# A delta-rule attention kernel: the inner outputs of six chunks by pairs of batches, their masks on GpSimd

## The chip, the cores and the metric

The kernel runs on one core of a Trainium2 chip. The metric is the device time of one execution in microseconds (us); the time given for a kernel is the median of several executions. A profile is one further execution, recorded by the hardware.

## The reference

Two stages. The first is a delta-rule attention over 4 batches, 8 heads, 768 steps and a head of 48:

```python
for t in range(S):
    kt, vt, bt = (k_n[:, :, t], v[:, :, t], beta[:, :, t, None])
    y[:, :, t] = np.einsum('bhd,bhde->bhe', q[:, :, t], state)
    v_old = np.einsum('bhde,bhd->bhe', state, kt)
    state = state + bt[:, :, :, None] * np.einsum('bhd,bhe->bhde', kt, vt - v_old)
```

(`k_n` are the keys divided by their norms.) The second stage takes the 3072 rows of 384 that come out, routes each to one of 16 experts (a group of 4 by argmax, then one of its 4), and computes `combined * (relu(x @ w1) @ w2)` with that expert's weights. Everything is float32.

## The kernel before

The attention is done in 24 chunks of 32 steps. All four batches are worked on at once: partition `b * 32 + t` holds step t of batch b. Within a chunk the recurrence is solved by the inverse of a triangular 32x32 matrix; such inverses are made on VectorE for a group of four chunks at a time (`inverse(g)`, lines 392 and 398 being its products and additions), transposed (L428), and spread into a factor `mtb` that is zero between the two batches of a pair (L437 on VectorE, L439 on ScalarE). Group g serves chunks 4g to 4g + 3; the last, group 5, is spread by VectorE alone.

Chunk u is `advance(u)`. On TensorE it multiplies the state with the keys (`a_ps`, L495) and with the queries (`o_ps`, L504), the factor with that (`w_ps`, L512), then updates the state (`s_ps`, L523), which ScalarE copies back in two pieces into `s_bd` (L529); the next chunk's `a_ps` waits for them. Last comes the inner output: the masked products of the chunk's queries and keys (`gq`) times `w`, added to `o_ps`; ScalarE copies the sum to `x` (L546). `logits(u - 1)` (L564, L465) turns the previous chunk's `x` and multiplies it with the router's weights, and `route` works on the logits of a group of chunks: on GpSimd `acc` (L613), the steps from `rk` to `cw` (L655 to L663), `what` (L701), `mine` (L706) and four `at` (L647), which TensorE uses one per chunk in the sorting matmul (L729).

The products of queries and keys are made by `gram` ten chunks ahead (`LEAD` = 10), so those of chunk 23 are made during chunk 13, and from chunk 14 (`LATE`) on TensorE has none left to make. `mask(u)` sets to zero what lies on or after the diagonal. For most chunks it writes 64 columns for each head, the chunk's own 32 and 32 zeros for the other batch of its pair, so that one matmul of 64x64 serves two batches (16 matmuls a chunk, L537). For chunks 14 to 19 (`halved`) it writes only the 32 (128x256 instead of 128x512, L294 instead of L298), and 32 matmuls of 32x32 are made (L542). All masks are VectorE's.

The transposed keys and queries of chunk u lie in `kqt_[u % 12]`, keys in half 0, queries in half 1; `load_kq(u + 12)` fills the buffer again at the end of period u, for the last time for chunk 23 in period 11.

The order of the instructions on every engine is that in which the program issues them: the main loop over `u` issues a period, and between its steps `work(n)` and `allow(...)` issue pieces of the inverses and of the routing. Nothing is reordered afterwards; an engine runs its own list in order and waits where an instruction needs another engine's result. A mask is issued at the start of the period before its chunk (`mask(u + 1)`).

The expert stage follows: TensorE takes the 16 experts one after another while their weights are loaded and rows are gathered and scattered by GpSimd's DMAs.

Of the kernel before, what the change touches and what calls it, by code (L numbers as in the profile page):

```python
# [9 lines left out]
F32 = mybir.dt.float32  # L10
I32 = mybir.dt.int32
AX = mybir.AxisListType
ALU = mybir.AluOpType
# [3 lines left out]
C = 32  # L17
RG = 4
# [48 lines left out]
def deltanet_then_moe(  # L67
# [13 lines left out]
    nc = tc.nc  # L81
    B, H, S, D = shape
    NP = H // 2
    NCH = S // C
# [15 lines left out]
    quads = [slice(b * C, (b + 1) * C) for b in range(B)]  # L100
    pairs = [slice(0, 64), slice(64, 128)]
# [9 lines left out]
    cut = {name: con[:, a:b] for name, (a, b) in const_at.items()}  # L111
# [65 lines left out]
    with ExitStack() as first:  # L177
        ap_ = first.enter_context(tc.tile_pool(name="attn", bufs=1))
        wk = first.enter_context(tc.tile_pool(name="wk", bufs=2))
# [10 lines left out]
        NB, NV = LEAD + 2, 3  # L190
        LATE, SMALL, KR = NCH - LEAD, NGR - 1, 64 + D
        ENDING = NCH - 2
        halved = range(LATE, SMALL * RG)
        kqt_ = [ap_.tile([128, 2, NP, 128], F32, name=f"kqt{i}") for i in range(NB)]
        kv_ = [ap_.tile([128, NP * KR + H * D], F32, name=f"kv{i}") for i in range(NV)]

        def load_kq(u, a=None):
            half = slice(0, 2) if a is None else slice(a, a + 1)
            nc.sync.dma_start(out=kqt_[u % NB][0:KR, half],
                              in_=kq_d[u].rearrange("p (a j t) -> p a j t", a=2, j=NP)[:, half])  # L200
# [36 lines left out]
        gts, raws, gqs, mts, norm, vhs, xs, turned_over = {}, {}, {}, {}, {}, {}, {}, set()  # L237
# [49 lines left out]
        def mask(u):  # L287

            like = [128, H, 2, C]
            gqm = wk.tile(like, F32, tag="gqm", name=f"gqm{u}", bufs=3)  # L290
            if u in halved:
                gqs[u] = gqm.rearrange("p h a t -> p (h a t)")[:, 0:H * C].rearrange(
                    "p (h t) -> p h t", t=C)
                nc.vector.tensor_tensor(gqs[u], raws.pop(u), cut["causal"][:, None, :].to_broadcast(  # L294
                    [128, H, C]), op=ALU.mult)
                return
            gqs[u] = gqm
            nc.vector.tensor_tensor(  # L298
                gqs[u], raws.pop(u)[:, :, None, :].to_broadcast(like),
                cut["upper"].rearrange("p (a t) -> p a t", a=2)[:, None].to_broadcast(like),  # L300
                op=ALU.mult)
# [182 lines left out]
        def advance(u):  # L484

            g, uu = divmod(u, RG)
            kqt = kqt_[u % NB]
            k = kv_[u % NV][:, 0:NP * KR].rearrange("p (j d) -> p j d", j=NP)
            if u == 0:
                f = vhs.pop(u)  # L490
            else:
                a_ps = begun_with.pop(u)
                for j in range(NP):
                    for b in range(B):
                        nc.tensor.matmul(a_ps[quads[b], 2 * j:2 * j + 2, :],  # L495
                                         lhsT=kqt[0:KR, 0, j, quads[b]], rhs=s_bd[0:KR, b, j],
                                         start=False, stop=True, skip_group_check=True)
                f = wk.tile([128, H, D], F32, tag="f", name=f"f{u}")
                nc.scalar.activation(f, a_ps, ACT.Copy)
            o_ps = ps.tile([128, H, D], F32, tag="o", name=f"o_ps{u}")  # L500
            if u > 0:
                for j in range(NP):
                    for b in range(B):
                        nc.tensor.matmul(o_ps[quads[b], 2 * j:2 * j + 2, :],  # L504
                                         lhsT=kqt[0:KR, 1, j, quads[b]], rhs=s_bd[0:KR, b, j],
                                         start=(j == 0), stop=False, skip_group_check=True)
            yield
            mt = mts[g]
            w_ps = ps.tile([128, H, D], F32, tag="s", name=f"w_ps{u}")
            for h in range(H):  # L510
                for b in pairs:
                    nc.tensor.matmul(w_ps[b, h], lhsT=mt[b, uu * H + (h % 2) * NP + h // 2],  # L512
                                     rhs=f[b, h], start=(h == 0), stop=True,
                                     skip_group_check=True)
            w = wk.tile([128, H, D], F32, tag="w", name=f"w{u}")
            nc.scalar.activation(w, w_ps, ACT.Copy)
            yield


            if u < NCH - 1:  # L520
                for j in range(NP):
                    for b in range(B):
                        nc.tensor.matmul(s_at[0:KR, b, j], lhsT=k[quads[b], j, 0:KR],  # L523
                                         rhs=w[quads[b], 2 * j:2 * j + 2],
                                         start=(u == 0 and j == 0), stop=True,
                                         skip_group_check=True)
                for hh in range(2):
                    rows = slice(hh * 64, hh * 64 + D)
                    nc.scalar.activation(s_bd[rows, :, :, hh, :],  # L529
                                         s_at[rows, :, :, hh * D:(hh + 1) * D], ACT.Copy)  # L530
            yield
            gq = gqs.pop(u)
            for h in range(H):
                hq = (h % 2) * NP + h // 2
                if u not in halved:
                    for b in pairs:
                        nc.tensor.matmul(o_ps[b, h], lhsT=gq[b, hq].rearrange("p a t -> p (a t)"),  # L537
                                         rhs=w[b, h], start=(u == 0 and h == 0), stop=True,
                                         skip_group_check=True)
                else:  # L540
                    for b in range(B):
                        nc.tensor.matmul(o_ps[quads[b], h], lhsT=gq[quads[b], hq],  # L542
                                         rhs=w[quads[b], h], start=False, stop=True,
                                         skip_group_check=True)
            x = wk.tile([128, DM], F32, tag="x", name=f"x{u}", bufs=4)
            nc.scalar.activation(x, o_ps.rearrange("p h d -> p (h d)"), ACT.Copy)  # L546
            xs[u] = x
            yield
# [251 lines left out]
        with tc.manual_schedule(engines={mybir.EngineType.PE, mybir.EngineType.DVE,  # L800
# [34 lines left out]
            for n in (H * D, H * D):  # L835
                nc.tensor.matmul(s_ps[:, 0, 0:n], lhsT=ident, rhs=con[:, cols[1]:cols[1] + n],
                                 start=True, stop=True, skip_group_check=True)
            second = inverse(1)
            start(second, 0.95)
            while 0 not in mts:  # L840
                work(4)
                allow(ACT_STEP)
            mask(0)
            scale(1)
            allow(ROOTS)
# [50 lines left out]
            for u in range(NCH + 1):  # L896
                step = advance(u) if u < NCH else iter([None] * 4)
                turned = logits(u - 1) if u else iter([None] * 2)
                if 0 < u < NCH - 1:
                    mask(u + 1)  # L900
                if u == 2:
                    scale(RG)
# [80 lines left out]
                work(12)  # L983
                if u == 0:
                    mask(1)
                if 0 < u < NCH - NB:
                    load_kq(u + NB)
                if u < NCH - NV:
# [265 lines left out]
    with tc.For_i(0, n_over):  # L1254
# [23 lines left out]
                                op=ALU.mult)  # L1278
# [71 lines left out]
```

## Time and profile before

| | us |
|---|---|
| median of 3 executions | 498.28 (496.32 to 499.61) |
| profiled execution | 490.29 |
| its span (first to last instruction) | 488.5 |
| busy: TensorE | 446.1 (91%) |
| busy: VectorE | 241.9 (50%) |
| busy: ScalarE | 189.5 (39%) |
| busy: GpSimd | 187.1 (38%) |

In the profile PE is TensorE's matmuls, PEld its loading of weights, DVE VectorE, ACT ScalarE, POOL GpSimd; "issue" is time in which an engine waited for nothing that the profile shows. A float32 matmul of the program leaves two records on PE and two on PEld. The mean granted clock of TensorE was 0.994 of full speed. The chain of work that ended last passes through TensorE for 34% of the span, VectorE for 19%, DMA for 18%.

### The profile page before, as it was taken

What the parts mean: (1) busy time and instruction counts of PE and PEld (TensorE: products, weight loads), DVE (VectorE), ACT (ScalarE), POOL (GpSimd) and SP (SyncE); (2) the same over time, 40 slices, a digit from 0 to 9 for tenths busy, and PEclk for the clock granted to TensorE, in tenths of its full rate; (3) what the DMA queues carried; (4) which work ended last, traced back from release to release, by engine and by line L of the source; (5) the groups of instructions that cost most, each with busy time, mean ns of one, the idle gap of its engine ahead of it and who ended that gap; (6) DMA issues with size and microseconds to landing.
All of it is one profiled execution on the core that took longest, in us unless ns stands there. A gap on an engine that the chain in (4) does not pass through costs nothing.

```text
span 488.5 us, 18022 instructions
## 1 busy us (share of the span) xinstructions
PE 446.1 (91%) x7674; PEld 421.8 (86%) x7674; DVE 241.9 (50%) x890; ACT 189.5 (39%) x407; POOL 187.1 (38%) x322
## 2 busy tenths in 40 slices
PE   3447999989999999999999999999999999999992
PEld 3335888878888889889999999999999999999992
DVE  4999999999999995474101210220122011201110
ACT  2327888777877776532112111111211111111110
POOL 0040310634517124103455445545735365256122
PEclk9999999999999999999999999999999999999997
DMA  5567455444355542207977877958987898778740
GB/s 164 150 185 237 135 149 179 143 127 146 102 160 173 174 126 98 63 19 197 372 230 238 285 228 215 312 160 282 326 268 232 264 326 302 230 220 305 262 133 30
DMA packets 56741, 97.06 MB, mean 199 GB/s; under 512 B 18958, under 2 KB 41417, under 8 KB 56659
## 3 DMA queue, kind: packets, MB, share of 16 engines
q1 hardware_dynamic: 50739, 85.89, 55.3%
q0 software_dynamic: 5920, 10.00, 6.7%
q8 instruction: 61, 1.00, 0.9%
q14 instruction: 21, 0.17, 0.1%
HBM read 81.75 MB, written 14.27 MB: 197 GB/s over the span
## 4 chain that ended last, share of the span: by engine, by line
PE 34%; DVE 19%; DMA 18%; issue 12%; POOL 8%; ACT 4%; SPq 3%; POOLq 0%; DVEq 0%
PE h_ps L1115 7%; PE y_ps L1134 7%; DMA out_dram<-yo,to_i 7%; DMA y_dram<-yq 6%; POOL xq L1087 6%; DVE m L398 5%; DVE below L392 4%; PE w_ps L512 4%; DMA yr<-y_dram 4%; SPq L1174 2%; PE a_ps L495 2%; PE o_ps L537 2%; PE s_ps L523 2%; PE o_ps L504 2%; POOL out_dram L1146 2%
## 5 line engine op out<-in xcount | busy, mean ns | idle before, releaser
L1134 PE MATMUL y_ps<-hid,w 128*128 128x224 f32 (+15 forms) x768 | 132.2, 331 | 0.0
L1134 PEld LDWEIGHTS y_ps<-hid,w 128*128 128x128 f32 x768 | 129.0, 190 | 0.3
L1115 PE MATMUL h_ps<-xt,w 128*128 128x232 f32 (+14 forms) x720 | 122.7, 330 | 0.0
L1115 PEld LDWEIGHTS h_ps<-xt,w 128*128 128x128 f32 x720 | 120.1, 190 | 0.3
L1087 POOL DMA_INDIRECT xq<-x_dram,from_q x92 | 87.9, 955 | 34.7 <-issue 24.8
L1137 DVE COPY yt<-y_ps 128x232 f32<-128x232 f32 (+13 forms) x14 | 5.1, 366 | 133.3 <-PE y_ps L1134 133.3
L1118 ACT ACTIVATE hid<-h_ps 128x448 f32<-128x448 f32 (+15 forms) x64 | 32.1, 502 | 100.2 <-PE h_ps L1115 100.2
L1146 POOL DMA_INDIRECT out_dram<-yo,to_i x32 | 34.3, 1073 | 92.8 <-DVE yo L1184 82.1
L1139 ACT ACTIVATE yt<-y_ps 128x224 f32<-128x224 f32 (+15 forms) x34 | 11.4, 337 | 116.6 <-PE y_ps L1134 116.6
L398 DVE TENSOR_TENSOR m<-m,below 128x16 f32<-128x16 f32 (+4 forms) x180 | 53.6, 298 | 0.4
L392 DVE TENSOR_TENSOR below<-m 128x16 f32<-128x16 f32 (+4 forms) x180 | 52.1, 292 | 0.1
L529 ACT ACTIVATE s_bd<-s_ps 48x768 f32<-48x768 f32 x46 | 37.0, 805 | 5.4 <-PE s_ps L523 4.8
L1184 DVE TENSOR_SCALAR yo<-yr,gate 128x384 f32<-128x384 f32 (+14 forms) x28 | 11.2, 415 | 53.0 <-DMA yr<-y_dram 44.0
L512 PEld LDWEIGHTS w_ps<-f,mtb 64*64 64x64 f32 x736 | 23.5, 134 | 5.6 <-issue 2.7
L512 PE MATMUL w_ps<-f,mtb 64*64 64x48 f32 x736 | 26.7, 220 | 1.4 <-issue 0.9
L439 ACT ACTIVATE mtb<-mt,con 128x256 f32<-128x256 f32 x35 | 25.5, 744 | 1.1 <-DVE mt L428 1.1
L274 PE MATMUL g_ps<-kqt 48*32 48x64 f32 (+1 forms) x1152 | 16.8, 236 | 9.3 <-DMA kqt<-in_kq_dram 7.7
L523 PE MATMUL s_ps<-w,kv 32*112 32x96 f32 x736 | 24.3, 267 | 0.9 <-issue 0.5
L613 POOL TENSOR_TENSOR acc<-acc,hots 128x16 f32<-128x16 f32 x16 | 4.2, 260 | 53.1 <-DVE hots L611 52.1
L537 PE MATMUL o_ps<-w,gqm 64*64 64x48 f32 x576 | 21.2, 220 | 3.2 <-issue 3.1
L523 PEld LDWEIGHTS s_ps<-w,kv 32*112 32x112 f32 x736 | 20.4, 172 | 3.2 <-issue 0.7
L274 PEld LDWEIGHTS g_ps<-kqt 48*32 48x32 f32 x1152 | 13.4, 114 | 11.0 <-issue 6.6
(186 smaller groups left out, 581.8 us busy)
## 6 DMA issues: line engine op xcount, KB each, us to landing
w<-in_w_dram SPq DMA_DIRECT2D x29, 1536.0 KB, 8.3
kv<-in_kv_dram SPq DMA_DIRECT2D x24, 416.0 KB, 3.8
kqt<-in_kq_dram SPq DMA_DIRECT2D x20, 448.0 KB, 4.4
x_dram<-x SPq DMA_DIRECT2D x24, 192.0 KB, 2.5
w<-in_w_dram SPq DMA_DIRECT2D x24, 128.0 KB, 3.1
y_dram<-yq SPq DMA_DIRECT2D x36, 84.0 KB, 9.7
yr<-y_dram SPq DMA_DIRECT2D x14, 192.0 KB, 2.4
kqt<-in_kq_dram SPq DMA_DIRECT2D x8, 224.0 KB, 3.3
```

The lines of the kernel that those rows point to most:

```text
L274: nc.tensor.matmul(g_out[quads[b], hh * NP + j, of], lhsT=kqt[rows, 0, j, quads[b]], rhs=kqt[rows, of, j, quads[b]], start=True, stop=True ...
L392: nc.vector.tensor_tensor(t, column.to_broadcast(like), row.to_broadcast(like), op=ALU.mult)
L398: nc.vector.tensor_tensor(to, to, t, op=ALU.add)
L512: nc.tensor.matmul(w_ps[b, h], lhsT=mt[b, uu * H + (h % 2) * NP + h // 2], rhs=f[b, h], start=(h == 0), stop=True, skip_group_check=True)
L523: nc.tensor.matmul(s_at[0:KR, b, j], lhsT=k[quads[b], j, 0:KR], rhs=w[quads[b], 2 * j:2 * j + 2], start=(u == 0 and j == 0), stop=True, sk ...
L529: nc.scalar.activation(s_bd[rows, :, :, hh, :], s_at[rows, :, :, hh * D:(hh + 1) * D], ACT.Copy)
L537: nc.tensor.matmul(o_ps[b, h], lhsT=gq[b, hq].rearrange("p a t -> p (a t)"), rhs=w[b, h], start=(u == 0 and h == 0), stop=True, skip_group ...
L1087: nc.gpsimd.indirect_dma_start(out=xq[:, g, :], out_offset=None, in_=x_dram[:, :].rearrange("n (q c) -> (n q) c", q=4), in_offset=bass.Ind ...
L1115: nc.tensor.matmul(h_ps[:, k], lhsT=w1[:, j, (f + k) * 128:(f + k + 1) * 128], rhs=xt[:, j, 0:R], start=(j == 0), stop=(j == DC - 1), skip ...
L1118: nc.scalar.activation(hid[:, f:f + 2], h_ps, ACT.Relu)
L1134: nc.tensor.matmul(y_ps, lhsT=w2[:, f, j * 128:(j + 1) * 128], rhs=hid[:, f], start=(f == 0), stop=(f == FC - 1))
L1146: put = nc.gpsimd.indirect_dma_start(out=out[:, :], out_offset=bass.IndirectOffsetOnAxis(ap=to[0:P, i:i + 1], axis=0), in_=yo[0:P, :], in_ ...
```

## The change

For chunks 14 to 19 the masks get the full width of 128x512, are made by GpSimd instead of VectorE, and are issued at the end of the period two before their chunk. They are written into the key half of `kqt_[(u - 2) % 12]`, the buffer of chunk u - 2, into which nothing is loaded any more. The inner outputs of these chunks are made like those of the others, by 16 matmuls of 64x64.

```diff
-        halved = range(LATE, SMALL * RG)
+        ahead_masks, SOONER = range(LATE, SMALL * RG), 2
...
         def mask(u):
             like = [128, H, 2, C]
-            gqm = wk.tile(like, F32, tag="gqm", name=f"gqm{u}", bufs=3)
-            if u in halved:
-                gqs[u] = gqm.rearrange("p h a t -> p (h a t)")[:, 0:H * C].rearrange(
-                    "p (h t) -> p h t", t=C)
-                nc.vector.tensor_tensor(gqs[u], raws.pop(u), cut["causal"][:, None, :].to_broadcast(
-                    [128, H, C]), op=ALU.mult)
-                return
+            by_pool = u in ahead_masks
+            if by_pool:
+                gqm = kqt_[(u - SOONER) % NB][:, 0].rearrange("p j t -> p (j t)").rearrange(
+                    "p (h a t) -> p h a t", h=H, a=2)
+            else:
+                gqm = wk.tile(like, F32, tag="gqm", name=f"gqm{u}", bufs=3)
             gqs[u] = gqm
-            nc.vector.tensor_tensor(
+            (nc.gpsimd if by_pool else nc.vector).tensor_tensor(
                 gqs[u], raws.pop(u)[:, :, None, :].to_broadcast(like),
                 cut["upper"].rearrange("p (a t) -> p a t", a=2)[:, None].to_broadcast(like),
                 op=ALU.mult)
...
-                if u not in halved:
-                    for b in pairs:
-                        nc.tensor.matmul(o_ps[b, h], lhsT=gq[b, hq].rearrange("p a t -> p (a t)"),
...
-                else:
-                    for b in range(B):
-                        nc.tensor.matmul(o_ps[quads[b], h], lhsT=gq[quads[b], hq],
-                                         rhs=w[quads[b], h], start=False, stop=True,
-                                         skip_group_check=True)
+                for b in pairs:
+                    nc.tensor.matmul(o_ps[b, h], lhsT=gq[b, hq].rearrange("p a t -> p (a t)"),
...
-                if 0 < u < NCH - 1:
+                if 0 < u < NCH - 1 and u + 1 not in ahead_masks:
                     mask(u + 1)
...
                 work(12)
                 if u == 0:
                     mask(1)
+                if u + SOONER in ahead_masks:
+                    mask(u + SOONER)
```

GpSimd's order around two of the new masks, before: the last of the small steps of `route` for chunks 12 to 15, then what follows until the next `acc`.

```order
L663 TENSOR_TENSOR cw_3803<-sums_3801,cw_3803 128x4
L701 TENSOR_TENSOR what_3807<-what,half_3805 128x24
L706 TENSOR_TENSOR mine_3804<-hots,what_3807 128x384
L647 TENSOR_SCALAR at_4008<-con,low_3806 128x128
L647 TENSOR_SCALAR at_4010<-con,low_3806 128x128
L647 TENSOR_SCALAR at_4100<-con,low_3806 128x128
L647 TENSOR_SCALAR at_4274<-con,low_3806 128x128
L613 TENSOR_TENSOR acc<-acc,hots 128x16 x4
```

And in the changed kernel, whose line numbers are smaller by up to 7; the buffers `kqt_107` to `kqt_110` take the masks of chunks 16 to 19:

```order
L656 TENSOR_TENSOR cw_3785<-sums_3783,cw_3785 128x4
L297 TENSOR_TENSOR kqt_107<-gq_2126,con 128x512
L694 TENSOR_TENSOR what_3789<-what,half_3787 128x24
L699 TENSOR_TENSOR mine_3786<-hots,what_3789 128x384
L640 TENSOR_SCALAR at_3973<-con,low_3788 128x128
L640 TENSOR_SCALAR at_3975<-con,low_3788 128x128
L297 TENSOR_TENSOR kqt_108<-gq_2336,con 128x512
L640 TENSOR_SCALAR at_4064<-con,low_3788 128x128
L297 TENSOR_TENSOR kqt_109<-gq_2530,con 128x512
L640 TENSOR_SCALAR at_4221<-con,low_3788 128x128
L606 TENSOR_TENSOR acc<-acc,hots 128x16 x4
L297 TENSOR_TENSOR kqt_110<-gq_2724,con 128x512
```

Mask 16 now stands ahead of `what`, `mine` and the first `at`, masks 17 and 18 between later `at`, mask 19 behind `acc`. Mask 14 stands in the same way ahead of the fourth `at` of the group before; mask 15 lies behind GpSimd's part of inverse 5, a run of 14 small steps on `r` that ends with `nrm`, and ahead of the first of the small steps of `route`, `rk`:

```order
L333 TENSOR_TENSOR r_3629<-r_3629,m_3619 128x32
L334 TENSOR_SCALAR nrm_3627<-r_3629 128x32
L297 TENSOR_TENSOR kqt_106<-gq_1907,con 128x512
L648 TENSOR_TENSOR rk_3780<-rk_3780,hots 128x64
L649 TENSOR_TENSOR sx_3475<-sx_3475 128x20x2
```

VectorE's order loses the six masks and nothing else. At the first of them, mask 14 among the last products of inverse 4 before its second half, before the change:

```order
L392 TENSOR_TENSOR corner_14_3416<-m_2798 128x28
L392 TENSOR_TENSOR below_14_3418<-m_2798 128x224
L294 TENSOR_TENSOR gqm_3426<-gq_1716,con 128x256
L398 TENSOR_TENSOR m_2798<-m_2798,corner_14_3416 128x2x14
L597 TENSOR_REDUCE best_3473<-lg_2642 128x20
```

In the changed kernel the row of `gqm` is gone and the others follow each other as they stand. TensorE's order stays too; the row `L542 MATMUL o_ps_3679<-w_3723,gqm_3426 32x48 x32` of chunk 14 becomes `L535 MATMUL o_ps_3677<-w_3721,kqt_105 64x48 x16`, and likewise for the five chunks after it. ScalarE's and SyncE's lists are the same.

More of the change, by code (lines that the diff above doesn't have):

```diff
@@ L534, in advance @@
                 hq = (h % 2) * NP + h // 2
-                if u not in halved:
-                    for b in pairs:
-                        nc.tensor.matmul(o_ps[b, h], lhsT=gq[b, hq].rearrange("p a t -> p (a t)"),
-                                         rhs=w[b, h], start=(u == 0 and h == 0), stop=True,
-                                         skip_group_check=True)
-                else:
-                    for b in range(B):
-                        nc.tensor.matmul(o_ps[quads[b], h], lhsT=gq[quads[b], hq],
-                                         rhs=w[quads[b], h], start=False, stop=True,
-                                         skip_group_check=True)
+                for b in pairs:
+                    nc.tensor.matmul(o_ps[b, h], lhsT=gq[b, hq].rearrange("p a t -> p (a t)"),
+                                     rhs=w[b, h], start=(u == 0 and h == 0), stop=True,
+                                     skip_group_check=True)
             x = wk.tile([128, DM], F32, tag="x", name=f"x{u}", bufs=4)
```

## The prediction

> **What bounds the kernel now.** I read the page's table of slices first, to find the stage, then the table of windows, then the chain of work that ended last, and the engines' timelines last.
>
> ```profile
> DVE  4999999999999995474101210220122011201110
> ...
> core 0: us, PE busy (x) PEld busy (x) DVE busy (x) ACT busy (x) POOL busy (x), PEclk, DMA share, GB/s
> 146.30:186.50 40.20, 37.79 (x1227) 33.28 (x1226) 39.89 (x156) 29.26 (x60) 17.22 (x49) 1.00 0.52 159
> 216.80:488.50 271.70, 262.77 (x1618) 261.43 (x1605) 48.69 (x100) 44.29 (x101) 126.41 (x141) 0.99 0.75 244
> ```
>
> A slice is 12.2 us. VectorE is nearly always busy in slices 2 to 15 (the attention); in the experts' window behind them TensorE is (262.77 of 271.70 us) and VectorE is not. The change touches chunks 14 to 19, the window from 146.3 to 186.5: 40.2 of 488.5 us. The experts' 271.7 us stay as they are. In the window VectorE is busy for 39.89 of 40.20 us, so whatever is added to it delays all that follows on it. Whether this costs time is told by the chain. Its pieces are start, length and work.
>
> ```profile
> 180.54 1.01 PE s_ps L523 x32
> ...
> 181.58 0.77 ACT s_bd L529
> ...
> 182.39 0.82 ACT s_bd L529
> ...
> 183.25 0.87 PE a_ps L495 x32
> ...
> 186.60 0.97 PE s_ps L523 x32
> 187.57 0.78 PE l_ps L465 x6
> 188.35 1.06 PE o_ps L537 x32
> 189.41 0.80 PE a_ps L495 x32
> ...
> 192.69 0.97 PE s_ps L523 x32
> ```
>
> The first block is chunk 19 (quarters of 32x32), the second chunk 20, which already multiplies by pairs. In chunk 19 the chain leaves TensorE for ScalarE's two copies of the state (L529): the inner output lies in their shadow. In chunk 20 TensorE itself is the chain. VectorE is not on the chain in either: it is full, but ahead of those who wait for it. By how much is the point of this prediction.
>
> **TensorE: quarters to pairs.** Each matmul of the program leaves two records.
>
> ```profile
> L537 PE MATMUL o_ps<-w,gqm 64*64 64x48 f32 x576 | 21.2, 220 | 3.2 <-issue 3.1
> L542 PE MATMUL o_ps<-w,gqm 32*32 32x48 f32 x384 | 5.6, 203 | 0.7 <-issue 0.7
> ```
>
> Pairs halve the count, but not the time: a chunk's 32 records by pairs take 21.2/18 = 1.18 us, its 64 records by quarters 5.6/6 = 0.93 us, since four quarters run side by side and only two pairs. On the chain: from state update to state update chunk 19 takes 186.60 - 180.54 = 6.06 us and chunk 20 takes 192.69 - 186.60 = 6.09 us. From s_ps to a_ps it is 2.71 against 2.81, and 0.07 of that comes back because a_ps then follows without a gap (0.80 for 0.87). So pairs cost +0.03 us a chunk, six times: **+0.2 us**. Bounds: 0, if it stays in the shadow, and 6 x 0.10 = 0.6.
>
> **VectorE: six masks gone.** A mask by quarters lasts 0.41 us, but what it takes from VectorE is the distance to the next start:
>
> ```profile
> L294 DVE TENSOR_TENSOR gqm<-gq,con 128x256 f32<-128x256 f32 x6 | 2.6, 428 | 0.0
> ...
> 167.94 0.41 DVE L294 TENSOR_TENSOR gqm<-gq,con 128x256 f32<-128x256 f32 x1
> 168.28 0.18 DVE L398 TENSOR_TENSOR m<-m,corner 128x28 f32<-128x28 f32 x1
> ```
>
> 0.34 us each, 2.0 us in all.
>
> **GpSimd: six masks of 128x512 added.** No such row exists. The nearest form on GpSimd is `mine` (L706: two inputs, one of them spread out), and the mask of 128x512 itself on VectorE:
>
> ```profile
> L706 POOL TENSOR_TENSOR mine<-hots,what x4: 878/882/907, 98.2 to 184.3; 128x384 f32<-128x384 f32 x4
> L706 DVE TENSOR_TENSOR mine<-hots,what x1: 558/558/558, 198.4 to 198.4; 128x384 f32<-128x384 f32 x1
> L298 DVE TENSOR_TENSOR gqm<-gq,con 128x512 f32<-128x512 f32 x18 | 12.4, 691 | 0.0
> L647 POOL TENSOR_SCALAR at<-con,low 128x128 f32<-128x128 f32 x16 | 12.3, 780 | 0.0
> ```
>
> GpSimd takes 882/558 = 1.58 times VectorE for `mine`, so 691 x 1.58 = 1.09 us for a mask; by size 882 x 512/384 = 1.18 us. I take **1.15 us**. The ends are 0.69 us (no slower than VectorE) and 3.12 us (four times the 780 ns of an `at` of 128 columns); `mine` is the nearest, being the same operation.
>
> **What a GpSimd product does to VectorE.** The same step of two inverses, without GpSimd and with `mine` beside it:
>
> ```profile
> 69.50 0.21 DVE L398 TENSOR_TENSOR m<-m,corner 128x52 f32<-128x52 f32 x1
> ...
> 156.82 0.88 POOL L706 TENSOR_TENSOR mine<-hots,what 128x384 f32<-128x384 f32 x1
> 156.93 0.84 DVE L398 TENSOR_TENSOR m<-m,corner 128x52 f32<-128x52 f32 x1
> ...
> 157.69 2.97 POOL L647 TENSOR_SCALAR at<-con,low 128x128 f32<-128x128 f32 x4
> 158.07 0.20 DVE L392 TENSOR_TENSOR below<-m 128x48 f32<-128x48 f32 x1
> ```
>
> The step lasts 0.84 instead of 0.21 us and ends with `mine`: VectorE lost 0.63 of its 0.88 us. So a mask of 1.15 us takes some 0.90 us from VectorE and gives back 0.34. Five masks meet the inverse's two-input products: 5 x 0.56 = 2.8 us. Mask 15 meets the end of inverse 4 (a reciprocal, one product, a transpose), where I take 0.5 - 0.34 = 0.2. **VectorE ends up 3.0 us later, not 2.0 us earlier**, when it has made the spread factor of chunk 20. Bounds: -2.0 (no clash) and 6 x (3.12 - 0.25 - 0.34) = +15.2 us.
>
> The Trainium skill's page "SBUF — State Buffer", section "Who interferes with whom", says that a VectorE instruction with two SBUF inputs and a GpSimd instruction that reads SBUF exclude each other, and that the loser stands still for the whole instruction. With `mine` the trace agrees (0.84 for 0.21 us). Beside the four `at`, which read SBUF too, it does not: the row at 158.07 has its usual 0.20 us. By the page's rule all six masks would cost VectorE time; if a mask behaved as an `at`, none would, which is the first rival.
>
> **Who waits for VectorE.** Chunk 20 is the first that needs inverse 5:
>
> ```profile
> 181.48 0.78 DVE L437 TENSOR_SCALAR mtb<-mt,con 128x256 f32<-128x256 f32 x2
> 184.79 1.01 PEld L512 LDWEIGHTS w_ps<-f,mtb 64*64 64x64 f32 x32 [0.23 <-ACT f L499]
> ```
>
> The two halves of its factor end at 181.48 + 0.78 = 182.26 and are used at 184.79: 2.5 us of cover. With 3.0 us of delay they are ready at 185.3. TensorE comes there at 184.79 + 0.2 (pairs) + 0.2 (below) = 185.2. I count **+0.2 us**, between 0 and, by the far bound, 15.2 - 2.5 = 12.7 us.
>
> **The queue of GpSimd.** It runs in order, so a mask waits behind what was issued before it, and what follows waits for the mask.
>
> ```profile
> 128.79 2.97 POOL L647 TENSOR_SCALAR at<-con,low 128x128 f32<-128x128 f32 x4
> 151.52 0.59 POOL L335 TENSOR_SCALAR nrm<-r 128x32 f32<-128x32 f32 x1
> 152.19 0.37 POOL L655 TENSOR_TENSOR rk<-rk,hots 128x64 f32<-128x64 f32 x1
> 154.37 0.25 POOL L663 TENSOR_TENSOR cw<-sums,cw 128x4 f32<-128x4 f32 x1
> 154.97 0.77 PEld L542 LDWEIGHTS o_ps<-w,gqm 32*32 32x32 f32 x64
> 156.52 0.23 POOL L701 TENSOR_TENSOR what<-what,half 128x24 f32<-128x24 f32 x1 [1.90 <-DVE below L392]
> 159.84 0.30 PEld L729 LDWEIGHTS s_ps<-mine,at 128*128 128x128 f32 x2
> 171.04 1.20 POOL L613 TENSOR_TENSOR acc<-acc,hots 128x16 f32<-128x16 f32 x4 [10.38 <-DVE hots L611]
> ```
>
> Mask 14 stands behind three of the four `at` at 128.79 and ends near 132.5, two chunks ahead of its use. Mask 15 stands behind the roots of inverse 5, which end with `nrm` at 152.11; mask 14 has delayed VectorE, and so the roots, by 0.56. It runs from 152.7 to 153.8, and chunk 15 reads it at 154.97: 1.1 us to spare, not two periods. Behind it the eight small steps `rk` to `cw` take 154.62 - 152.19 = 2.4 us, to 156.3, then mask 16 until 157.4. `what` then also waits for VectorE's reciprocal, about 1.3 us later than now, and runs at 157.8; `mine` ends at 159.0, the first `at` at 159.75. TensorE wants it at 159.84. Nominally that fits by 0.1 us; I count **+0.2 us**, between 0 and 1.0 (should each of the two masks take 0.4 us longer). Masks 17 and 18 stand between later `at`, mask 19 behind `acc`, which now ends at 172.2; with VectorE's 2.5 us mask 19 is done by 176, its use comes after the state update that ScalarE copies at 181.6. No DMA is issued or moved, and the key buffers taken over have their last readers, a_ps and o_ps, at the start of the period at whose end the mask is issued.
>
> **Where TensorE pauses.** Two pauses inside a run of equal matmuls lie in the window:
>
> ```profile
> 159.19 0.43 PE L512 MATMUL w_ps<-f,mtb 64*64 64x48 f32 x8 [0.65 <-issue]
> 176.32 0.36 PE L542 MATMUL o_ps<-w,gqm 32*32 32x48 f32 x11 [0.75 <-issue]
> ...
> 159.19:176.32 17.13, 15.94 (x510) 13.96 (x511) 17.10 (x84) 13.67 (x26) 2.44 (x7) 1.00 0.61 188
> ```
>
> They stand 510 matmuls and as many weight loads apart, and nothing that the profile shows releases them: I read them as instruction fetch. The change drops 6 x 32 = 192 matmuls and their loads, 0.38 of such a distance. The pauses move to other matmuls: 0.7 us less if one falls where TensorE waits anyway, 0.7 us more if one leaves such a place. I take **0**. The page "Runtime: NRT & Kernel Launch" of the Trainium skill, section "Instruction fetch mechanics", calls crossing a block of 256 instructions mostly hidden; here some crossing in every 1020 instructions is not, at 0.65 and 0.75 us. By the page the term would be 0 as well, but without its bounds.
>
> **Sum.** 0.2 + 0.2 + 0.2 + 0 = +0.6 us. The profiled execution took 490.29 us (1.8 us around its span), so it would take 490.9. The timed runs are 496.32 to 499.61 us with a median of 498.28; the difference carried over gives **498.9 us**, no change that can be told: a measurement of this kernel tells about 1% (5 us) from nothing.
>
> **Rivals.**
> 1. *No clash*: a mask costs VectorE nothing, as an `at`. VectorE runs 2.0 us earlier, nobody waited for it, and the pairs' 0.2 us remain, with up to 0.7 us won by the pauses: -0.5 to +0.2, about 498.1 us. Against it stands `mine`, with the mask's own operation. 0.15.
> 2. *Late behind the roots*: mask 15 misses chunk 15, or the `at` behind mask 16 its sorting matmul, so that a GpSimd wait takes the chain: +1 to +2.5 us, some 500 us. For it speak spare times of 1.1 and 0.1 us. 0.12.
> 3. *Slower: VectorE falls behind.* If GpSimd needs far longer for the mask, inverse 5 comes too late and TensorE stands before w_ps of chunk 20. With a mask of x us the wait is 6 (x - 0.59) - 2.5: it begins at x = 1.0, passes 5 us at x = 1.84, and at the 3.12 us of the `at` rate gives 12.7 us, 511 us. For it: an `at` takes 6.1 ns a column against 2.3 of `mine`. Against it: an `at` is another operation. 0.05.
> 4. *The gain is larger than any row shows* (more than 5 us). The six inner outputs take 5.6 us of TensorE in all, mostly in shadow; it would have to come from elsewhere. 0.02.
>
> The forecast (0 to +1.2) keeps 0.66. **The range**: the lowest timed run less 0.7 for the pauses, 495.6, to the highest plus 2.2 (of rival 2), 501.8. It leaves out rivals 3 and 4 and the tails of the timing. Chances: faster by over 1% 0.03 (rival 4 and timing), slower 0.06 (rival 3 and timing), within 1% 0.91.
>
> **What would show it.** Right: GpSimd masks of 1.1 to 1.2 us; beside each a VectorE product stretched to 0.8 us or more; TensorE's o_ps of chunks 14 to 19 by 32 records in 1.06 us and a period longer by 0.03; the factor of chunk 20 later relative to TensorE, its cover of 2.5 us gone or nearly. Wrong: masks above 1.8 us, w_ps of chunk 20 waiting for VectorE for microseconds, o_ps of chunk 15 waiting for GpSimd, or the pauses adding up differently by more than one.

## The result: 1.1% slower, and the profile after

| | before | changed |
|---|---|---|
| median of 20 executions, us | 496.01 (491.32 to 499.73) | 500.27 (495.41 to 502.57) |
| ratio | | 1.0113, 95% interval 1.0088 to 1.0139 (+5.6 us) |
| profiled execution, us | 490.29 | 502.16 |
| first expert matmul starts at | 218.1 | 226.7 |

The ratio, like every ratio below, leaves out executions that took over 1.5% longer than the fastest of their kernel; the profiled execution of e5, below, was such a one and is not read. The time lies in the range that was forecast, 1.4 us above the 498.9. The loss of 1.13% lies just outside the case "within 1%", which had a chance of 0.91, though its interval begins inside it. And the agreement in time hides a miss: the difference was forecast as 0.6 us, and it is nine times that. (The three times before that the forecast started from have a median 2.3 us above that of the 20.)

The profiled executions differ by 11.9 us, more than the medians do. Before the first expert matmul 8.6 us of that are lost, between chunks 20 and 22; most of the rest is a wait for expert weights that the profile before did not have, and that another execution of the changed kernel, below, had hardly (0.2 us):

```profile
PE h_ps L1110 <- DMA w<-in_w_dram: 1.9, 2, 1.7
```

So the place to look at is the end of the attention. First the table of windows of the changed kernel, with the prediction's window and four short ones behind it:

```profile
core 0: us, PE busy (x) PEld busy (x) DVE busy (x) ACT busy (x) POOL busy (x), PEclk, DMA share, GB/s
146.30:186.50 40.20, 37.05 (x1008) 33.28 (x1004) 39.76 (x140) 29.88 (x60) 21.43 (x50) 1.00 0.54 162
...
184.00:188.00 4.00, 1.87 (x78) 1.68 (x68) 3.90 (x13) 0.49 (x1) 0.01 (x1) 1.00 0.20 75
188.00:192.00 4.00, 2.00 (x24) 1.54 (x23) 3.53 (x7) 1.35 (x3) 3.92 (x5) 0.68 0.01 4
192.00:196.00 4.00, 4.00 (x62) 3.79 (x56) 0.81 (x4) 1.79 (x3) 1.07 (x2) 0.50 0.36 107
196.00:200.00 4.00, 4.00 (x95) 3.63 (x94) 2.53 (x10) 0.98 (x2) 0.00 (x0) 0.54 0.15 53
```

GpSimd has 4.2 us more in the large window (21.43 for 17.22). Behind it TensorE is busy for only 3.87 of 8 us, and then fully busy for 8 us at a granted clock of about half. Before the change TensorE was busy for 3.99 to 4.00 us in each of these four short windows, at a clock of 1.00. TensorE's timeline shows what it does there, and what it waits for:

```profile
180.52 1.04 PE L522 MATMUL s_ps<-w,kv 32*112 32x96 f32 x32
...
187.05 1.13 PE L511 MATMUL w_ps<-f,mtb 64*64 64x48 f32 x32 [2.13 <-DVE half L685]
...
190.66 0.75 PE L722 MATMUL s_ps<-mine,at 128*128 128x96 f32 x2 [2.00 <-POOL at L640]
191.33 1.82 PE L522 MATMUL s_ps<-w,kv 32*112 32x96 f32 x32
...
201.06 1.04 PE L522 MATMUL s_ps<-w,kv 32*112 32x96 f32 x32
```

From the state update of chunk 19 to that of chunk 20 it takes 10.8 us (6.06 before), with two waits, for VectorE and for GpSimd; from there to chunk 21's 9.7 us (6.09 before), without any wait, but with nearly every group of matmuls up to 199 us almost twice as long: the state update of chunk 20 lasts 1.82 instead of 1.04 us. That is 4.8 + 3.6 = 8.4 us. In the chain of work that ended last VectorE now carries the stretch from 154 to 188 us; its last pieces there, and how the chain gets back to TensorE:

```profile
184.26 1.25 DVE mt L427
...
187.99 0.80 POOL what L694
...
189.74 0.87 POOL at L640
...
190.66 0.75 PE s_ps L722 x2
191.40 1.75 PE s_ps L522 x32
```

Now the steps upstream. The masks on GpSimd, and one of them with VectorE's product beside it and the next of its kind:

```profile
L297 POOL TENSOR_TENSOR kqt<-gq,con x6: 1272/1278/1369, 130.7 to 175.9; 128x512 f32<-128x512 f32 x6
...
175.92 1.28 POOL L297 TENSOR_TENSOR kqt<-gq,con 128x512 f32<-128x512 f32 x1
175.99 1.31 DVE L397 TENSOR_TENSOR m<-m,below 128x80 f32<-128x80 f32 x1
177.41 0.24 DVE L397 TENSOR_TENSOR m<-m,below 128x96 f32<-128x96 f32 x1
```

A mask takes 1.28 us, and a product that takes some 0.2 us lasts 1.31 and ends with it: VectorE loses 1.1 us a mask. Mask 15 holds it too, and there the held instruction is a copy with one input, which took 0.13 us before (the first row of the kernel before, below):

```profile
152.72 1.27 POOL L297 TENSOR_TENSOR kqt<-gq,con 128x512 f32<-128x512 f32 x1
152.94 1.10 DVE L424 COPY m<-r 128x32 f32<-128x32 f32 x1
```

Last VectorE's transposes of inverse 4 and of inverse 5, and what follows the second, in the kernel before:

```profile
152.56 0.13 DVE L425 COPY m<-r 128x32 f32<-128x32 f32 x1
...
152.79 1.25 DVE L428 STREAM_TRANSPOSE mt<-m 128x1024 f32<-128x1024 f32 x1
...
179.61 1.25 DVE L428 STREAM_TRANSPOSE mt<-m 128x1024 f32<-128x1024 f32 x1
183.10 0.18 DVE L697 RECIPROCAL what<-cw 128x4 f32<-128x4 f32 x1
185.14 3.35 POOL L647 TENSOR_SCALAR at<-con,low 128x128 f32<-128x128 f32 x4
186.24 0.36 PE L729 MATMUL s_ps<-mine,at 128*128 128x96 f32 x2
```

and in the changed one:

```profile
154.15 1.25 DVE L427 STREAM_TRANSPOSE mt<-m 128x1024 f32<-128x1024 f32 x1
...
184.26 1.25 DVE L427 STREAM_TRANSPOSE mt<-m 128x1024 f32<-128x1024 f32 x1
187.74 0.17 DVE L690 RECIPROCAL what<-cw 128x4 f32<-128x4 f32 x1
187.99 0.80 POOL L694 TENSOR_TENSOR what<-what,half 128x24 f32<-128x24 f32 x1 [7.46 <-DVE what L690]
188.86 0.89 POOL L699 TENSOR_TENSOR mine<-hots,what 128x384 f32<-128x384 f32 x1
189.74 3.33 POOL L640 TENSOR_SCALAR at<-con,low 128x128 f32<-128x128 f32 x4
```

VectorE transposes inverse 5 4.65 us later: 1.36 of it are there at inverse 4 (masks 14 and 15, and what this execution had lost by then), and the time from one transpose to the other has grown from 26.82 to 30.11 us, by 3.29, for the four masks between (4 x (1.1 - 0.34) = 3.0). Everything behind it moves by as much: the reciprocal, GpSimd's `what` and `mine`, and the first `at`, which TensorE's sorting matmul of this same chunk 20 needs. Before the change the first of the four `at` ended near 186.0 and was used at 186.24: a cover of some 0.2 us, against 2.5 us for the factor. VectorE's 4.65 us less such a cover is what the matmul lost: it began at 190.66, 4.42 us later.

### The profile page after: what moved, and what is told of

The parts are those of the page before. It is cut to its first block, busy times and chain, and to the rows that moved or that the text cites. A ratio compares the mean times of both kernels' runs of the same rounds, so it can differ in the third digit from the quotient of the medians.

```text
span 500.4 us, 17647 instructions
## 1 busy us (share of the span) xinstructions
PE 455.1 (91%) x7482; PEld 430.4 (86%) x7482; DVE 246.6 (49%) x884; ACT 189.7 (38%) x407; POOL 195.0 (39%) x328
## 4 chain that ended last, share of the span: by engine, by line
PE 64%; issue 8%; DMA 8%; DVE 7%; ACT 6%; SPq 3%; POOL 3%; POOLq 0%; DVEq 0%; ACTq 0%
PE h_ps L1110 19%; PE y_ps L1129 19%; DMA kqt<-in_kq_dram 4%; PE o_ps L535 4%; PE w_ps L511 4%; PE l_ps L464 3%; PE a_ps L494 3%; DVE m L397 3%; PE s_ps L522 2%; PE o_ps L503 2%; DMA yr<-y_dram 2%; DMA y_dram<-yq 2%; SPq L1173 2%; PE t_ps L557 2%; POOL out_dram L1141 1%
## 5 line engine op out<-in xcount | busy, mean ns | idle before, releaser
L397 DVE TENSOR_TENSOR m<-m,below 128x16 f32<-128x16 f32 (+4 forms) x180 | 55.9, 310 | 0.4
L522 PE MATMUL s_ps<-w,kv 32*112 32x96 f32 x736 | 26.2, 279 | 0.5 <-ACT found L865 0.3
L522 PEld LDWEIGHTS s_ps<-w,kv 32*112 32x112 f32 x736 | 22.0, 183 | 3.1 <-issue 0.8
L535 PE MATMUL o_ps<-w,gqm 64*64 64x48 f32 x576 | 22.6, 230 | 2.2 <-issue 2.1
L397 DVE TENSOR_TENSOR m<-m,corner 128x28 f32<-128x28 f32 (+6 forms) x84 | 23.9, 284 | 0.0
```

What stands on the lines that cost most here:

```text
L397: nc.vector.tensor_tensor(to, to, t, op=ALU.add)
```

## The experiments

Two theories were set against each other at the outset. **Clash**: the two-input products on GpSimd hold VectorE, and its lateness makes TensorE wait in chunk 20. **TensorE's own work**: pairs, the order of the matmuls, or fetch pauses moved by 192 matmuls. A third came up with the windows above: how much of the loss is the **halved clock** that follows the wait. Ratios are to the kernel before on the same chip. The column on VectorE is the time between the transposes of inverses 4 and 5, each from one profiled execution. As a gauge of VectorE it does not carry what an execution lost earlier: the kernel before shows 26.82 and, in an execution that was late by then, 26.72. The last two columns are when the transpose of inverse 5 and the sorting matmul of chunk 20 began. e9 to e11, which change TensorE's order, are left to their own paragraph.

| kernel | ratio (95%) | VectorE, transpose 4 to 5, us | transpose 5, us | sorting matmul of chunk 20, us |
|---|---|---|---|---|
| before, first profile | 1 | 26.82 | 179.61 | 186.24 |
| before, again (e14) | | 26.72 | 181.97 | 195.47 |
| e1, pairs, masks by VectorE | 1.0008 (0.9975 to 1.0042) | 27.85 | 180.72 | 187.11 |
| e3, idle one-input GpSimd work | 1.0013 (0.9986 to 1.0039) | 28.66 | 182.10 | 188.52 |
| e5, three masks by GpSimd | 1.0043 (1.0001 to 1.0084) | | | |
| e4, changed, TensorE kept busy | 1.0064 (1.0032 to 1.0097) | 30.03 | 184.51 | 190.93 |
| e12, masks by one-input selections | 1.0105 (1.0068 to 1.0143) | 30.80 | 185.40 | 191.81 |
| changed | 1.0113 (1.0088 to 1.0139) | 30.11 | 184.26 | 190.66 |
| changed, again (e13) | 1.0128 (1.0073 to 1.0183) | 29.78 | 185.68 | 192.09 |
| e2, idle two-input GpSimd products | 1.0142 (1.0109 to 1.0175) | 31.12 | 186.55 | 192.94 |
| e8, idle VectorE products | 1.0163 (1.0116 to 1.0210) | 29.88 | 184.08 | 190.50 |

Up to 28.7 us nothing that can be told is lost; from 29.8 us on every kernel loses 0.6% or more. In all eight profiles below the two of the kernel before TensorE waited there for `at`, and the sorting matmul began 6.39 to 6.42 us after the transpose. In the first profile before it began 6.63 us after and did not wait: a cover of 0.23 us. In that chunk VectorE sets the time. What a wait there costs is harder to tell, as e1 shows.

**Pairs alone (e1).** The changed kernel, with all masks made by VectorE.

```diff
-        ahead_masks, SOONER = range(LATE, SMALL * RG), 2
+        ahead_masks, SOONER = range(0), 2
```

> The pairs alone: chunks 14 to 19 by 16 matmuls of 64x64, their masks of 128x512 by VectorE at the usual place, GpSimd as before. Theory (GpSimd's products hold VectorE, inverse 5 comes late, TensorE waits and its clock is halved): VectorE loses only 6 x 0.26 = 1.6 us, inside its 2.5 us of cover, so no wait before w_ps of chunk 20, full clock from 188 to 200 us, and a time within 0.3% of before. Rival (pairs cost more on TensorE than the rows show): slower by 0.5 to 1%, with no change on VectorE.

The ratio is 1.0008: pairs, 192 matmul records fewer and moved pauses cost nothing that can be told, which rules out the second theory as the source of the loss. The profile was not as expected, for TensorE did wait in chunk 20, and the halved clock followed:

```profile
183.50 1.14 PE L511 MATMUL w_ps<-f,mtb 64*64 64x48 f32 x32 [1.18 <-DVE half L685]
187.11 0.74 PE L722 MATMUL s_ps<-mine,at 128*128 128x96 f32 x2 [2.00 <-POOL at L640]
...
184.00:188.00 4.00, 2.00 (x31) 1.54 (x31) 3.98 (x9) 1.35 (x3) 3.48 (x4) 0.70 0.00 0
188.00:192.00 4.00, 4.00 (x58) 3.78 (x60) 0.43 (x2) 1.79 (x3) 1.53 (x3) 0.50 0.31 87
192.00:196.00 4.00, 4.00 (x94) 3.63 (x90) 2.93 (x12) 0.98 (x2) 0.00 (x0) 0.52 0.21 77
```

TensorE came 2.5 us earlier here (state update of chunk 19 at 177.98) and stood until its inputs were ready at a time near the old one. A wait's length is thus no measure of a loss. Nor is the halved clock: these windows lack 0.30 + 0.50 + 0.48 of 4 us, 5.1 us, as much as the changed kernel's (0.32 + 0.50 + 0.46), and the state update of chunk 21 came at 197.40, against 192.62 in the first profile before. Yet the timed executions lose nothing. The profiled execution took 494.12 us, near the 493.85 that the kernel before has as its median on the same chip, while the first profile before, at 490.29, lies 5.7 us below its own median; executions of the kernel before may often have such a wait, which two profiles of it can't tell. What does separate e1 and e3 from the kernels that lose is when VectorE transposes inverse 5: at 180.7 and 182.1 us, against 184.1 to 186.6.

**Idle GpSimd products on the old kernel (e2), and idle GpSimd scalings in the same places (e3).** The kernel before computes as it did; GpSimd additionally writes six results that nobody reads into the key buffers, by the mask's own operation or by a scaling of the same size with one input.

```diff
+                if u + 2 in halved:
+                    ...
+                    nc.gpsimd.tensor_tensor(spare, raws[u + 2]..., cut["upper"]..., op=ALU.mult)      # e2
+                    nc.gpsimd.tensor_scalar(spare, raws[u + 2]..., 1.0, None, op0=ALU.mult)           # e3
```

> The suspected cost alone: the kernel before, quarters and VectorE's masks kept, plus six products of 128x512 on GpSimd at the places of the change, into the same key buffers; nobody reads them. Theory: each holds a VectorE product for 1.1 us (1.3 instead of 0.2), VectorE comes 6 to 7 us late to inverse 5, TensorE waits 3 to 5 us there, the clock is halved for some 10 us, and the kernel is slower than before by 1.2 to 2%. Rival (pairs, or fewer instructions on TensorE, cause the loss): no change.

> As the run with six idle products, but each GpSimd instruction has one input (a scaling of the same 128x512 by 1.0). Theory: one-input instructions do not hold VectorE (as the four at of before), so VectorE comes on time, and the time is within 0.3% of before, even if GpSimd takes 1 to 3 us for each. Rival (GpSimd's queue is what comes late, whatever the instruction): slower by 0.4 to 1%, with waits of TensorE for at.

The products alone bring the whole loss, 1.0142, the scalings none, 1.0013, although they last longer. Beside each a VectorE product of 128x80, in e2 and then in e3:

```profile
178.11 1.28 POOL L990 TENSOR_TENSOR kqt<-gq,con 128x512 f32<-128x512 f32 x1
178.19 1.30 DVE L398 TENSOR_TENSOR m<-m,below 128x80 f32<-128x80 f32 x1
```

```profile
174.34 1.49 POOL L990 TENSOR_SCALAR kqt<-gq 128x512 f32<-128x512 f32 x1
174.40 0.64 DVE L398 TENSOR_TENSOR m<-m,below 128x80 f32<-128x80 f32 x1
```

A two-input product holds VectorE for its whole length, a scaling of 1.49 us for 0.4 us (0.64 for the 0.23 of the same step before). The four scalings between the transposes make VectorE 1.8 us late (28.66 for 26.82). That is more than the 0.2 us of cover, and e3's profile has a wait of 1.69 us for `at` in chunk 20; but no loss that can be told comes of it.

**VectorE late without GpSimd (e8).** Eight idle products of 128x512 on VectorE in periods 13 to 18 of the kernel before.

```diff
+                if u + 1 in halved:
+                    ...
+                    for _ in range(1 + (u % 4 == 1)):
+                        nc.vector.tensor_tensor(spare, raws[u + 1]..., cut["upper"]..., op=ALU.mult)
```

> The lateness alone, without GpSimd and without pairs: the kernel before with eight idle products of 128x512 added on VectorE at the start of periods 13 to 18 (two in 13 and 17), 8 x 0.6 = 4.8 us. Theory (what costs is that VectorE comes late to inverse 5 and to the routing of chunks 12 to 15): TensorE waits some 4 us in chunk 20, for w_ps and for the first at, its clock is halved behind that, and the kernel is slower than before by 0.8 to 1.4%, like the changed kernel. Rival (GpSimd's own queue, or the pairs): less than 0.3%.

VectorE takes as long between the transposes as in the changed kernel, 29.88 us, and the loss is there: 1.0163. GpSimd need not take part; VectorE's lateness is enough.

**Half the dose (e5).** Masks 14 to 16 by GpSimd, 17 to 19 by VectorE (`range(LATE, LATE + 3)`).

> Half the dose: masks 14, 15 and 16 by GpSimd as in the change, masks 17, 18 and 19 by VectorE at 128x512, pairs in all six chunks. Theory: VectorE loses 3 x (1.1 - 0.34) + 3 x 0.26 = 3.1 us instead of 4.6; the result lies between the pairs alone (0.1% slower than before) and the changed kernel (1.1%): 0.4 to 0.9%. Rival (a threshold: no loss until some cover is used up): below 0.3%.

1.0043, as expected, and in keeping with a cost that grows with the number of GpSimd masks; but the interval reaches from nearly nothing to most of the loss.

**TensorE kept busy while it waits (e4).** The changed kernel with 16 idle matmuls in chunk 20, where it waited.

```diff
+        def fill(n):
+            for _ in range(n):
+                nc.tensor.matmul(s_ps[...], lhsT=ident, rhs=ident[:, 0:32], ...)
...
+            if u == SMALL * RG:
+                fill(8)          # ahead of w_ps, and again ahead of the sorting matmul
```

> The changed kernel with 8 matmuls of 128x128 by 32 columns, into columns that nobody reads, before w_ps of chunk 20 and 8 more before its sorting matmul, so that TensorE is busy while it waits. Theory (the wait itself costs some 4 us, and the halved clock behind it about as much again): the waits for VectorE and for at remain, the clock stays at 1.0 from 188 to 200 us, and the kernel is 3 to 4 us faster than the changed one: slower than before by 0.2 to 0.6%. Rival (the clock drops for another reason): as the changed kernel, 1.1% slower than before, clock 0.5 again.

The loss falls to 1.0064, though the inputs are no earlier (sorting matmul at 190.93):

```profile
188.00:192.00 4.00, 3.70 (x49) 3.37 (x49) 3.80 (x9) 1.35 (x3) 3.67 (x4) 0.90 0.02 4
192.00:196.00 4.00, 4.00 (x62) 3.79 (x60) 0.75 (x4) 1.80 (x3) 1.34 (x3) 0.50 0.34 107
196.00:200.00 4.00, 4.00 (x109) 3.71 (x108) 2.59 (x10) 1.18 (x3) 0.00 (x0) 0.75 0.16 53
```

The clock still falls, though TensorE was busy for 4.00 of 4 us from 184 to 188 and for 3.70 in the first row, so the standing of TensorE is not all that brings it down. But it falls for less: the three windows lack 0.10 + 0.50 + 0.25 of 4 us, 3.4 us, where the changed kernel lacked 5.1 us. This speaks for a part of the loss being the clock and not the wait, about half by the ratios. It is not shown: the intervals overlap, this ratio was not taken on the same chip as the changed kernel's, and e1 has the 5.1 us without a loss.

**Taking the wait out of the order (e9 to e11).** The sorting matmul of chunk 20 is left to chunk 22's, where the rest are done: in the changed kernel (e9), in the one before (e10), and in the one before with quarters in chunks 1 to 23 (e11).

```diff
-                if later:
+                if later and u != SMALL * RG:          # e9, e10, e11
...
-        halved = range(LATE, SMALL * RG)
+        halved = range(1, NCH)                          # e11 alone
```

> The changed kernel, but chunk 20 makes no sorting matmul; those of its group move by one chunk and the last is made with the others in chunk 22. Theory (the sorting matmul of chunk 20 has 0.15 us of cover, w_ps of chunk 20 has 2.5): the wait for at goes, the wait of about 2 us before w_ps stays, and less or nothing of the halved clock follows: 2 to 5 us faster than the changed kernel, slower than before by 0.1 to 0.7%. Rival (only the late inverse counts, the wait for at would be taken up by another): as the changed kernel.

> The kernel before with the same shift of the sorting matmuls. Theory: in its profiled execution TensorE did not wait there, so nothing, or up to 0.5% faster if most executions of it do wait and lose clock in chunk 20. Rival: no change in any case.

> The opposite of the change: quarters and masks of 128x256 by VectorE in chunks 1 to 23, with the shifted sorting matmuls. By the rows: VectorE gains 17 x 0.26 = 4.4 us, TensorE 17 x 0.2 = 3.4 us where the inner output is not in ScalarE's shadow, less some 1 us for 17 x 128 more instructions to fetch: faster than before by 0.2 to 0.8%. Rival (fetch pauses take it back): no change or slower.

None gained what the clash theory expected. e10 is slower than the kernel before (1.0058, interval 1.0017 to 1.0098), though its VectorE is on time (26.74 us between the transposes): the block of sorting matmuls at the end grows, and from the state update of chunk 21 to the next it takes 9.5 us instead of 8.3, which is 1.2 of the 2.9 us. e9 stays at 1.0162 (1.0106 to 1.0218). Its profile has no wait in chunk 20 and no halved clock behind it; but there TensorE itself came late (state update of chunk 19 at 184.94) after spells of halved clock between 48 and 60, 92 and 100, and 124 and 132 us, so that it met a VectorE as slow as the changed kernel's (29.89 us) without a wait. Why the timed executions gain nothing is open. e11 is the slowest, 1.0286 (1.0242 to 1.0330), some 14 us, and the rival of fetch pauses was right in the main: by its table of waits, 12.5 us go to pauses of the three rows below that nothing releases. With L537 it is 13.8 us, where the inner outputs, `w_ps` and L504 of the kernel before have 4.7.

```profile
PE o_ps L542 <- issue: 5.7, 11, 0.8
PE w_ps L512 <- issue: 4.3, 5, 1.1
PE o_ps L504 <- issue: 2.5, 2, 1.3
```

**Masks on GpSimd with one input (e12).** The kernel before with its quarters, the six masks made by GpSimd with four selections of 32x256 each, two periods ahead.

```diff
+                for q in quads:
+                    nc.gpsimd.affine_select(gqs[u][q], raw[q], pattern=[[0, H], [1, C]],
+                                            compare_op=ALU.is_gt, fill=0.0, base=0, channel_multiplier=-1)
```

> Masks on GpSimd that read one tensor: quarters as before, but masks 14 to 19 are four affine selections of 32 partitions by 256 columns each on GpSimd, two periods ahead, into the key buffers. Theory: one-input instructions do not hold VectorE, which gains 6 x 0.34 = 2.0 us: between no change and 0.5% faster than before, and VectorE's first routing reciprocal for chunks 12 to 15 comes some 2 us earlier. Rival (anything added to GpSimd's queue makes the routing late): slower by 0.3% or more.

1.0105 (1.0068 to 1.0143), slower and not faster. VectorE's timeline at two places beside selections (a mask of four selections begins at 163.83 us and ends at 166.11):

```profile
159.31 0.18 DVE L703 RECIPROCAL what<-cw 128x4 f32<-128x4 f32 x1 [1.06 <-POOL cw L669]
...
164.56 0.47 DVE L398 TENSOR_TENSOR below<-m 128x96 f32<-128x96 f32 x1
...
165.14 0.48 DVE L404 TENSOR_TENSOR m<-m,below 128x96 f32<-128x96 f32 x1
```

Each of the four selections of a mask holds one product by some 0.2 us (0.47 and 0.48 for the 0.24 of the same steps before), 0.9 us a mask, hardly less than the one GpSimd product does; and the longer queue makes VectorE stand for 1.06 us where the reciprocal waits for `cw`, which is the rival's mechanism. Four masks give 4 x (0.9 - 0.34) = 2.2 us, with the wait 3.3 of the 4.0 us (30.80 for 26.82) that VectorE takes longer.

**Both kernels again (e13, e14).** To see how far one profile stands for a kernel.

> The changed kernel again, beside the others on one chip. Theory: 1.0 to 1.4% slower than before, VectorE 4 to 5 us late at the transpose of inverse 5, a wait and a halved clock near 190 us.

> The kernel before, one more profile, to see how its first profiled execution (490.29 us, clock 0.994) stands to others (clock 0.98). Theory (VectorE sets when chunk 20 can go on): the transpose of inverse 5 near 180 us again; TensorE halved for some 10 us at one or two other places.

The changed kernel again waits 2.0 us for `at` and 0.4 for the factor in chunk 20, with the clock at half from 191 to 201 us. The kernel before took 499.30 us in its one execution, with no wait of TensorE for VectorE or GpSimd, but with spells of halved clock at 44 to 62, 116 to 120 and 177 to 188 us, of which these are two windows:

```profile
180.00:184.00 4.00, 4.00 (x98) 3.79 (x98) 3.58 (x7) 2.04 (x4) 0.00 (x0) 0.50 0.33 105
184.00:188.00 4.00, 4.00 (x86) 3.54 (x80) 1.89 (x8) 1.36 (x4) 2.07 (x5) 0.52 0.17 57
```

Its TensorE came to chunk 20 so late that the first `at` had been ready for some 4 us, and its first expert matmul began at 227.4 us, later than the changed kernel's at 226.7. So halved clock is no invention of the change, the first profile before, without any such spell ahead of 440 us, was an unusually clean one, and the 8.6 us by which the first pair of profiles differs there are not the price of the change. Over the timed executions it is nevertheless mostly the slower kernels that have the lower clock: the median of the mean granted clock is 0.982 to 0.986 before, 0.979 in e3, 0.977 in e1, but 0.969 to 0.973 in the changed kernel and 0.970 in e2; e8, with the largest loss of these, has 0.975. Between 0.984 and 0.969 lie 1.5% of some 490 us, 7 us of full clock, of which what falls into waits costs nothing; e13 lost 6.3 us. Clock and loss go together, which does not say by itself which brings which.

## Why the prediction was right and where it was not

**The mechanism was right as far as VectorE.** That a mask on GpSimd would stretch VectorE's products as `mine` does, and that TensorE would meet a late VectorE in chunk 20, is what the trace shows. e2 and e3 confirm the first by itself, and e8 that VectorE's lateness alone brings the loss. That the time fell into the range is luck all the same: the range got its width from the scatter of the timed executions, and the forecast of no change that can be told was off by nine times. (Its upper end adds 2.2 us for rival 2, which the rival itself puts at up to 2.5.)

**Pairs: right.** Expected 0.2 us, and e1 shows none that can be told. The inner outputs run as forecast, at about the length of the rows of the other chunks (6.8/6 = 1.13 us by 32 records, 1.18 forecast), and 192 records are gone:

```profile
L535 PE MATMUL o_ps<-w,gqm 64*64 64x48 f32 x576 | 22.6, 230 | 2.2 <-issue 2.1
L535 PE MATMUL o_ps<-w,kqt 64*64 64x48 f32 x192 | 6.8, 220 | 0.0
```

**The queue of GpSimd: right within its bounds.** Mask 15 ran at 152.72, forecast 152.7, and chunk 15 did not wait. Mask 16 followed `cw`, and the first `at` began at 159.91, 0.9 us later than forecast for it. In chunk 16 TensorE waited for it, as rival 2 had feared, by 0.72 us where the sum has 0.2 and the bound 1.0:

```profile
160.58 0.46 PE L722 MATMUL s_ps<-mine,at 128*128 128x96 f32 x2 [0.72 <-POOL at L640]
```

Little came of it, for the kernel before has a pause of 0.65 us in the same chunk (159.19): from the state update of chunk 15 to that of chunk 16 it takes 7.24 us after and 7.01 before. In e13 there is no such wait.

**The size of the hold: too small.** Forecast 1.15 us a mask and 0.90 us of it lost; measured 1.28 and 1.1. For mask 15 the prediction took 0.5 us; it was 1.0 (1.10 for 0.13). With the 2.0 us given back, the forecast lateness was 3.0 us and the measured one 4.65 in these two executions, of which some 3 between the transposes stand in both profiles of the changed kernel (29.78 and 30.11, for 26.72 and 26.82).

**The cover: the step that failed.** The prediction followed VectorE's lateness to one consumer, the spread factor (2.5 us of cover), and stopped. The reciprocal stands in the same VectorE list behind the factor, and behind it `what`, `mine` and the first `at`, which chunk 20's own sorting matmul used some 0.2 us after it was made. The prediction had looked at that chain only for chunk 16. "+0.2 us" for chunk 20 became 4.8 us in the profiled pair.

**What follows a wait: not in the sum.** The sum ended with the wait, at full clock. From the state update of chunk 20 to 199.7 us the work ran at half clock, 3.6 us more in the profiled pair. Whether this is a part of the cost stays open: e4 speaks for it, e1 against it. So does how the 5.6 us come about in the median execution, for a wait in chunk 20 stands in e1 and e3 too, which lose nothing, and e9 took the sorting matmul out of that chunk and gained nothing. Shown is that VectorE's lateness brings the loss, and not by which wait.

**The rivals.** Rival 3 named the mechanism that decided (VectorE falls behind, a wait ahead of w_ps), but gave it a chance of 0.05 because it asked for masks above 1.84 us before the loss would pass 5 us. With 1.28 us its formula gives 6 (1.28 - 0.59) - 2.5 = 1.6 us; the trace's w_ps wait was 2.13. In e13 that wait was 0.40. The formula is near for the wait that it described, and lacked the second wait and the clock.

No run beat the kernel before; e1 and e3 can't be told from it.

## What to carry to other kernels

Where an engine is full but not on the chain, its lead over every consumer is the budget of a change, and it has to be read for each of them down to the last one that TensorE waits for: with the smallest cover the waiting begins (here 0.2 us behind four steps of two engines), not with the first that one finds. What the wait costs is for timed executions to say: e1 and e3 have it for nothing that can be told. A two-input product moved to GpSimd beside a VectorE that is never idle is paid by VectorE at full length, so that moving 0.34 us off it cost it 1.1. And behind every wait of TensorE in chunk 20 that was profiled here stood a spell of halved clock, which a sum that ends with the wait leaves out; its price was not settled here.

## What the runs showed of the hardware

**GpSimd can be starved for long.** In e2 the first idle product, 1.28 us elsewhere, stood for 6.38 us while VectorE ran 23 products without a gap; only then was one VectorE product held, for 1.42:

```profile
132.44 6.38 POOL L990 TENSOR_TENSOR kqt<-gq,con 128x512 f32<-128x512 f32 x1 [0.73 <-PE a_ps L495]
...
137.60 1.42 DVE L398 TENSOR_TENSOR m<-m,below 128x176 f32<-128x176 f32 x1
```

The Trainium skill's page "SBUF — State Buffer", section "Who interferes with whom", says that the order of issue decides who blocks, for a whole instruction; here the loser lost to many instructions in a row. A one-input `at` met the same in e3: it stood for 5.09 us, from 162.81 on, where others take some 0.7.

**One-input work takes part in the clash, on both sides.** A one-input copy on VectorE was held (1.10 for 0.13 us, mask 15). A one-input instruction on GpSimd held VectorE once, for 0.2 us (a selection of 32x256) or 0.4 (a scaling of 128x512, of its 1.49 us), so that four short ones cost nearly as much as one two-input product. Nor is an `at` quite free, though the prediction had read it so from one row: the product `m<-m,below` of 128x80 lasted 0.32 us beside the `at` of the kernel before (at 160.19), and 0.24 with GpSimd idle (e2, at 131.98).

**The clock stays low long after the wait.** Between 184.9 and 190.7 us TensorE worked for about 1.6 us; the granted clock fell to half near 189.4 us (0.68 in 188 to 192) and came back near 199.7 (0.54 in 196 to 200), nine microseconds after TensorE had become busy again. The Trainium skill's page "TensorE: Matmul & The Clock Gate", section "What's actually happening", lets full clock return after one busy window of about 3.4 us; the trace does not agree, it took nearly three of them. From fall to return the clock was halved for 10.2 us here (twice the 5.1 us that it lacked). Behind the waits in chunk 20 of the other profiles it was 3.4 us (e8), 6.8 to 6.9 (e3, e4, e12) or again 10.2 (e1, e2, e13): one, two or three times 3.4 us, and the longest where TensorE had waited for the factor as well as for `at`.
